# A deeper buffer plan for two interleaved attentions, with the head split of Q moved by small DMAs

## The chip, the cores and the metric

The kernel runs on one core of one Trainium2 chip. Its engines are called PE (matmuls), ACT (exponentials and other functions), DVE (vector work), GpSimd (POOL in profiles) and SyncE (SP in profiles), which here only issues DMA transfers. The metric is the device time of one execution in microseconds (us), the median of several runs. All runs quoted here were in the same, undisturbed state; the granted TensorE clock of each is given where it matters.

## The reference

Two attentions on a sequence of 2048, width 512, 32 heads of 16; the outputs stand side by side. A works on four segments of 512 with a causal mask and a linear memory carried between segments; B is plain attention.

```python
# A, for each segment s of 4 (L = 512)
logits = einsum('bhqd,bhkd->bhqk', qs, ks) * scale + mask
a_dot  = einsum('bhqk,bhkd->bhqd', softmax(logits), vs)
a_mem  = (phi(qs) @ M) / (phi(qs) @ z + 1e-6)       # phi(t) = t+1 if t>0 else exp(t)
o      = g * a_mem + (1 - g) * a_dot                # g = sigmoid(beta), per head
M, z   = M + phi(ks).T @ vs, z + phi(ks).sum()
# B
p = softmax(einsum('bhqd,bhkd->bhqk', q, k) * Dh**-0.5)
o = einsum('bhqk,bhkd->bhqd', p, v)
# both: heads joined, times wo, concatenated on the last axis
```

B has 4 x 4 x 2 x 16 = 512 blocks of exponentials (chunks of queries, rows of heads, halves of a row, blocks of keys), each of four banks of 512 columns in PSUM, the memory that PE writes. B is the greater part of the work.

## The kernel before

The program schedules itself while it is built. It keeps a clock for each engine (`T["pe"]`, `T["dve"]`, `T["sp"]` and so on), prices every operation, and emits instructions in the order that this model gives. Projections, loads and memory updates are "chores" with a due place, an earliest time (`after`) and a condition (`ok`). So a changed rule or price reorders instructions everywhere.

ACT does most exponentials, two or three banks at a time, into "P buffers" (tile pT), from which PE multiplies them with V. Some blocks of B, the "V blocks", are done on DVE instead: four conversions out of PSUM (L938) and three additions (L954) per block, into a ring of buffers (tile vx).

```python
VBUFS = 9        # ring "vx" of the V blocks
VBACK = 1.5      # us of work that may wait for DVE before V scores are refused
PBUFS = 6        # buffers of exponentials
WARMTH = 0.52    # below this activity, PE gets multiplications with zeros

def load_xT(pool, name, ch, tag, bufs):              # x of a segment: four transposing DMAs, SyncE
    t = pool.tile([P, 4, W], BF16, name=f"xT_{name}", tag=tag, bufs=bufs)
    for cc in range(4):
        nc.sync.dma_start_transpose(t[:, cc, :], xs[name][ch * W:(ch + 1) * W, cc * P:(cc + 1) * P])
    return t

# in do_q: Q of two heads comes out of PSUM, then two GpSimd passes by a mask `par`
        def evac():
            qc = wk.tile([P, W], BF16, name="qc", tag="qc", bufs=2)
            pin(nc.vector.tensor_copy(qc[:], ps[:]))
            for e in range(2):
                pin(nc.gpsimd.tensor_scalar(dst[:, e, :], qc[:], par[:, e:e + 1], 0.0, ALU.mult, ALU.add))
                on_pool(0.8, T["dve"])
            mark(key, T["pool"])
# ...
        def seg_chores(s, rt):                        # projections of segment s of A, row of heads rt
            # ...
            def project():
                rel = T["sp"] + 3.5                   # when x is taken to be there
                if (s, rt) != (0, 0):
                    chore(d - LEAD, part(k()), 4, after=rel if s else ARRIVE[...],
                          key=("k", "a", s, rt), ok=lambda: s == 0 or ("phk", s - 1, rt) in seen)
                    chore(d - LEAD, part(q()), 4, after=rel if s else ARRIVE[...],
                          key=("q", "a", s, rt))
                # ... rt == 0: four chores for v
            def load():
                if s > 0:
                    xTA[s] = load_xT(wk, "a", s, "xTA", 1)
                    on_sp(4 * 1.3, T["pe"])
                # ...
                project()
            if rt == 0:
                chore(d - 18, load(), 1, slot=False, ok=...)
            else:
                project()                             # rows 1 to 3: at once, without load()

        def v_pick():                                 # may a block of B go to DVE?
            if vlive[0] > VBUFS - 2:
                return False
            # ...
        def v_scores(taken, lim=2, force=False):
            n = 0
            while n < lim and (force or backlog() < VBACK) and free_slots(...) and v_pick():
                # one score matmul into PSUM; later() queues L938, 0.685 us, on DVE,
                # and three additions L954, 0.70 us each

        def held_back(t):                             # a score step waits for its P buffer
            return pend.get(t - PBUFS, 0) > 0
```

All matmuls go through one helper (`mm`, line 117 of before), so in the profile they carry one line and are told apart by their tiles. PE, DVE, ACT and GpSimd run in program order; SyncE's DMAs are not pinned.

## Time and profile before

| before | value | from |
|---|---|---|
| time | 898.31 us, median of 3 (898.14 to 898.75) | runs |
| granted clock, profiled run | 0.997 | cores |
| ACT busy; exponentials from three or two banks | 868.2 of 896.6 us; 749 | busy times, groups |
| V blocks (512 blocks of B in all) | 124 | groups |
| splits of Q on GpSimd in the run | 28 | groups |

ACT's waits for scores, as the profile gives them (us in total, times, longest):

```profile
ACT pT L865 <- PE s_ps L117: 7.5, 12, 2.0
```

The busy time of one ACT instruction overlaps the next, though (in the changed kernel one starts at 180.60 us and runs 1.58 us, and the next starts at 181.93), so that "97% busy" does not say how near to its own fastest pace ACT runs.

### The profile page before, as it was taken

How to read it: one execution, taken by the hardware profiler on the slowest of the kernel's cores; microseconds unless marked ns; L12 is line 12 of the kernel's file. 1: busy time of each engine (PE TensorE's matmuls, PEld its weight loads, DVE VectorE, ACT ScalarE, POOL GpSimd, SP SyncE). 2: the span in 40 equal slices, each digit the busy share in tenths (PEclk: the TensorE clock that was granted, in tenths of full speed). 3: DMA queues.
4: the chain of work that ended last, by engine and by line, in shares of the span. 5: the costliest groups of instructions: out<-in, count | busy, mean ns of one | idle time of the engine just before them, and what ended most of it. 6: DMA issues, size and time to landing. Idle time of an engine off the chain costs nothing. (4 is left out here: it accounts for less than half of the span.)

```text
span 896.6 us, 18791 instructions
## 1 busy us (share of the span) xinstructions
PE 838.0 (93%) x7541; PEld 259.5 (29%) x7664; DVE 793.5 (88%) x1355; ACT 868.2 (97%) x779; POOL 156.8 (17%) x333
## 2 busy tenths in 40 slices
PE   8899999999999999999999999999999999999995
PEld 3222233322322222223332222223222222223221
DVE  4678799989798998999989998998999899999994
ACT  5999999999999999999999999999999999999995
POOL 5720300421403022031210404012040300000000
PEclk9999999999999999999999999999999999999998
DMA  9600000010000101000000010000000000000000
GB/s 205 129 9 13 18 2 7 7 30 2 7 1 19 37 7 26 1 1 7 2 7 1 20 36 1 1 1 1 2 2 1 14 30 7 1 2 1 1 2 29
DMA packets 36273, 15.48 MB, mean 17 GB/s; under 512 B 27984, under 2 KB 36176, under 8 KB 36176
## 3 DMA queue, kind: packets, MB, share of 16 engines
q1 hardware_dynamic: 34976, 13.78, 6.6%
q8 instruction: 62, 1.02, 0.5%
q10 hardware_dynamic: 1200, 0.39, 0.2%
q14 instruction: 35, 0.29, 0.1%
HBM read 4.20 MB, written 4.19 MB: 9 GB/s over the span
## 5 line engine op out<-in xcount | busy, mean ns | idle before, releaser
L865 ACT ACTIVATE pT<-s_ps 128x1536 bf16<-128x1536 f32 x749 | 856.2, 1292 | 9.9 <-PE s_ps L117 7.5
L938 DVE TENSOR_SCALAR vx<-v_ps 128x512 uint16<-128x512 f32 x496 | 323.3, 684 | 28.8 <-PE v_ps L117 23.8
L117 PE MATMUL s_ps<-qB,KB 32*128 32x512 bf16 x1552 | 251.7, 382 | 19.4 <-ACT pT L865 13.6
L954 DVE TENSOR_SCALAR vx<-vx 128x2048 uint16<-128x2048 uint16 x372 | 244.7, 693 | 2.1 <-PE acc L117 0.5
L117 PE MATMUL acc<-vx,VB 128*32 128x512 f16 x1984 | 178.0, 385 | 3.7 <-issue 2.3
L117 PE MATMUL v_ps<-qB,KB 32*128 32x512 bf16 x496 | 173.2, 382 | 3.5 <-DVE vx L938 1.1
L875 POOL TENSOR_SCALAR_AFFINE_SELECT pT<-pT 128x256 bf16<-128x256 bf16 (+2 forms) x241 | 105.5, 467 | 385.4 <-ACT pT L865 384.8
L117 PE MATMUL acc<-pT,VB 128*32 128x512 bf16 x1552 | 153.1, 387 | 0.7 <-DVE tT L374 0.5
L117 PEld LDWEIGHTS <-KB 32*128 32x128 bf16 x2048 | 84.6, 91 | 236.2 <-issue 229.3
L117 PEld LDWEIGHTS <-VB 128*32 128x32 bf16 x3536 | 73.1, 94 | 157.0 <-issue 146.1
L117 PE MATMUL acc<-zeros 128*128 128x512 bf16 x324 | 108.0, 385 | 3.5 <-issue 3.3
L374 DVE STREAM_TRANSPOSE tT<-acc 128x512 f32<-128x512 f32 x64 | 44.7, 703 | 17.0 <-PE acc L117 16.7
L117 PE MATMUL s_ps<-qA,kA 32*128 32x384 bf16 (+3 forms) x512 | 52.1, 299 | 8.0 <-ACT pT L865 6.2
L117 PEld LDWEIGHTS <-zeros 128*128 128x128 bf16 x420 | 34.0, 98 | 83.9 <-issue 76.2
L274 POOL TENSOR_SCALAR qA<-qc,par 128x512 bf16<-128x512 bf16 x24 | 18.9, 800 | 150.0 <-DVE qc L272 150.0
L117 PE MATMUL acc<-pT,vA 128*32 128x256 bf16 (+3 forms) x512 | 33.1, 305 | 2.9 <-POOL pT L875 1.2
L117 PEld LDWEIGHTS <-kA 32*128 32x128 bf16 x512 | 17.3, 91 | 47.5 <-issue 44.5
L274 POOL TENSOR_SCALAR qB<-qc,par 128x512 bf16<-128x512 bf16 x32 | 22.6, 716 | 14.8 <-DVE qc L272 14.8
L452 DVE CAST osb<-o_ps 128x512 bf16<-128x512 f32 x28 | 19.2, 686 | 5.9 <-PE o_ps L117 5.9
L408 POOL TENSOR_TENSOR tN<-tT,rsum 128x512 bf16<-128x512 f32 x1 | 1.4, 1367 | 130.5 <-DVE rsum L397 130.5
L272 DVE CAST qc<-q_ps 128x512 bf16<-128x512 f32 x28 | 19.1, 682 | 3.3 <-PE q_ps L117 2.6
L117 PE MATMUL k_ps<-xT_a,w_a 128*128 128x512 bf16 x59 | 18.5, 383 | 0.6 <-issue 0.6
(93 smaller groups left out, 425.4 us busy)
## 6 DMA issues: line engine op xcount, KB each, us to landing
out_dram<-osb SPq DMA_DIRECT2D x31, 128.0 KB, 1.7
w_b<-in_B_wqkv_dram SPq DMA_DIRECT2D x3, 512.0 KB, 5.0
phk<-phkT SPq DMA_TRANSPOSE x48, 2.4
w_a<-in_A_wv_dram SPq DMA_DIRECT2D x1, 512.0 KB, 4.5
wo_a<-in_A_wo_dram SPq DMA_DIRECT2D x1, 512.0 KB, 4.6
wo_b<-in_B_wo_dram SPq DMA_DIRECT2D x1, 512.0 KB, 5.3
xT_a<-in_A_x_dram SPq DMA_TRANSPOSE x16, 2.8
w_a<-in_A_wk_dram SPq DMA_DIRECT2D x1, 256.0 KB, 4.7
```

The source lines that it names most:

```text
L117: return pin(nc.tensor.matmul(out, lhsT, rhs, **k))
L272: pin(nc.vector.tensor_copy(qc[:], ps[:]))
L274: pin(nc.gpsimd.tensor_scalar(dst[:, e, :], qc[:], par[:, e:e + 1], 0.0, ALU.mult, ALU.add))
L374: pin(nc.vector.transpose(st["tT"][:, e].rearrange("p c d -> p (c d)"), acc[:]))
L408: pin(eng.tensor_tensor(o, tT[:, :, :, 0:DH], rr.to_broadcast(bc), op=ALU.mult))
L452: pin(nc.vector.tensor_copy(osb[:], ps[:]))
L865: pin(nc.scalar.activation(pT[:, 0:n, :], pt[:, 0:n, :], ACT.Exp, scale=SCALE))
L875: pin(nc.gpsimd.affine_select(out=blk, in_=blk, compare_op=ALU.is_ge, fill=0.0, base=0, pattern=[[0, len(sls)], [1, P]], channel_multiplie ...
L938: pin(nc.vector.tensor_scalar(x[:, j, :], vt[:], XSCALE, float(LADDER[0]), ALU.mult, ALU.add))
L954: pin(nc.vector.tensor_scalar(p[:], x[:], float(off - LADDER[0]), 32767.0, ALU.add, ALU.min))
```

## The change

Its intent: keep more V blocks going and keep GpSimd out of DVE's way. The V rule is relaxed (VBACK), the ring gets a tenth buffer and P buffers rise to eight; to pay for the memory, three of the four x chunks of B live in the ring only while keys and values are projected, and are loaded again for later Q. Q is split by eight small DMAs into tiles that were zeroed once, unless SyncE's queue is late.

```diff
-VBUFS = 9        +VBUFS = 10
-VBACK = 1.5      +VBACK = 1.8
-PBUFS = 6        +PBUFS = 8
-    bd = const.tile([P, 2, P], F32, name="bd")
+    bd = const.tile([P, 2, P], BF16, name="bd")
@@ do_q
-            for e in range(2):
-                pin(nc.gpsimd.tensor_scalar(dst[:, e, :], qc[:], par[:, e:e + 1], 0.0, ALU.mult, ALU.add))
-                on_pool(0.8, T["dve"])
-            mark(key, T["pool"])
+            if live[0] and T["sp"] < T["dve"] + 1.0:
+                for e in range(2):
+                    for j in range(4):
+                        r = slice(32 * j + DH * e, 32 * j + DH * e + DH)
+                        nc.sync.dma_start(out=dst[r, e, :], in_=qc[r, :])
+                        on_sp(0.5, T["dve"] + 0.1)
+                mark(key, T["sp"] + 2.2)
+            else:
+                ... as before
@@ x of B
-        xTB += [load_xT(wk, "b", ch, f"xTB{ch}", 1) for ch in range(1, 4)]
+        xTB += [load_xT(wk, "b", ch, "vx", VBUFS) for ch in range(1, 4)]
+            def again():
+                xTB[ch + 1] = load_xT(wk, "b", ch + 1, "xTB0", 1)
+                on_sp(4 * 1.3, T["pe"])
+                xat[ch + 1] = T["sp"] + 3.5
+            chore(..., q(), ..., ok=lambda: xat.get(ch, 1e9) < T["pe"])
... zeros 128 columns wide and broadcast; Q tiles zeroed once; vlive starts at 5; last store on ACT's queue
```

More of the change, by code (lines that the diff above doesn't have):

```diff
@@ L39 @@
 PREWARM = 16
-VBUFS = 9
+VBUFS = 10
 VMIN = 3
 VLATE = 0.5
-VBACK = 1.5
+VBACK = 1.8
 BANKS = (3, 2)
-PBUFS = 6
+PBUFS = 8
 SWITCH = 0.095
@@ L272, in evac @@
             pin(nc.vector.tensor_copy(qc[:], ps[:]))
-            for e in range(2):
-                pin(nc.gpsimd.tensor_scalar(dst[:, e, :], qc[:], par[:, e:e + 1], 0.0, ALU.mult, ALU.add))
-                on_pool(0.8, T["dve"])
-            mark(key, T["pool"])
+            if live[0] and T["sp"] < T["dve"] + 1.0:
[6 more added lines that the diff above has]
+            else:
+                for e in range(2):
+                    pin(nc.gpsimd.tensor_scalar(dst[:, e, :], qc[:], par[:, e:e + 1], 0.0, ALU.mult, ALU.add))
+                    on_pool(0.8, T["dve"])
+                mark(key, T["pool"])
             if phi is not None:
@@ L487 @@
         ld(nc.sync, 2)
-        xTB += [load_xT(wk, "b", ch, f"xTB{ch}", 1) for ch in range(1, 4)]
+        xTB += [load_xT(wk, "b", ch, "vx", VBUFS) for ch in range(1, 4)]
         woA = load_wo(big, "a", nc.sync)
         woB = load_wo(big, "b", nc.sync)
-        zeros = wk.tile([P, W], BF16, name="zeros")
+        zeros = wk.tile([P, 1, P], BF16, name="zeros")
         nc.gpsimd.memset(zeros[:], 0.0)
+        zcols = zeros[:].to_broadcast([P, 4, P])
         pre = mp.tile([P, W], F32, name="pre", tag="misc")
         for i in range(PREWARM):
-            mm(pre[:], zeros[:, 0:P], zeros[:], start=(i == 0), stop=(i == PREWARM - 1))
+            mm(pre[:], zeros[:, 0, :], zcols, start=(i == 0), stop=(i == PREWARM - 1))
         KB = big.tile([P, NRT, S], BF16, name="KB")
@@ L503 @@
         head_masks()
+        qz = {n: [wk.tile([P, 2, W], BF16, name=f"q{n}{rt}") for rt in range(NRT)] for n in "ab"}
+        for rt in range(NRT):
+            nc.gpsimd.memset(qz["b"][rt][:], 0.0)
         kA, qA, vA, phq, mbds, qB = {}, {}, {}, {}, {}, {}
@@ L537 @@
         okm = wk.tile([P, 2], BF16, name="okm")
-        chores, nchore, seen = [], [0], set()
+        chores, nchore, seen, xat, left_b = [], [0], set(), {0: 0.0}, [0]
         def place():
@@ L560, in q @@
             def q():
-                qA[s, rt] = wk.tile([P, 2, W], BF16, name="qA", tag=f"qA{rt}")
+                qA[s, rt] = qz["a"][rt]
                 if s > 0:
@@ L632, in bq_chores, with q, counted @@
         def bq_chores(ch, rt):
-            qB[ch, rt] = wk.tile([P, 2, W], BF16, name="qB", tag=f"qB{rt}")
-            chore(pos0["b", ch, rt] - LEAD - 1.5, do_q(mp, wk, wB, xTB[ch], rt, qB[ch, rt], None, ("q", "b", ch, rt)),
-                  after=ARRIVE["wvb"], key=("q", "b", ch, rt))
+            qB[ch, rt] = qz["b"][rt]
+            def q():
+                yield from do_q(mp, wk, wB, xTB[ch], rt, qB[ch, rt], None, ("q", "b", ch, rt))
+                if rt == NRT - 1 and ch < NSEG - 1:
+                    chore(pos0["b", ch, rt] - LEAD - 1.0, again(), 1, slot=False, ok=lambda: left_b[0] == 0)
+            def again():
+                xTB[ch + 1] = load_xT(wk, "b", ch + 1, "xTB0", 1)
+                on_sp(4 * 1.3, T["pe"])
+                xat[ch + 1] = T["sp"] + 3.5
+                return
+                yield
+            chore(pos0["b", ch, rt] - LEAD - 1.5, q(), after=ARRIVE["wvb"], key=("q", "b", ch, rt),
+                  ok=lambda: xat.get(ch, 1e9) < T["pe"])
         def b_kv_chores():
-            left = {"k": S // P, "v": S // P}
-            def counted(which, g):
+            left = {"k": S // P, "v": S // P, 1: 8, 2: 8, 3: 8}
+            left_b[0] = 2 * S // P
+            def counted(*keys, g):
                 yield from g
-                left[which] -= 1
-                vlive[0] -= left[which] == 0
+                left_b[0] -= 1
+                for k in keys:
+                    if k:
+                        left[k] -= 1
+                        vlive[0] -= left[k] == 0
             def ones():
@@ L652, in b_kv_chores @@
                     chore(pos0["b", 0, rt] - LEAD - (KLEAD if rt else 0) + 3 * ch,
-                          counted("k", do_k(mp, wB, xTB[ch], rt, KB[:, rt, ch * W:(ch + 1) * W], ("k", "b", ch, rt))),
+                          counted("k", ch, g=do_k(mp, wB, xTB[ch], rt, KB[:, rt, ch * W:(ch + 1) * W], ("k", "b", ch, rt))),
                           after=ARRIVE["xb"][ch], key=("k", "b", ch, rt))
             for sb in range(S // P):
-                chore(pos0["b", 0, 0] - 0.5 + 0.9 * sb, counted("v", do_v(
+                chore(pos0["b", 0, 0] - 0.5 + 0.9 * sb, counted("v", sb // 4, g=do_v(
                     mp, wB, xTB[sb // 4], sb % 4, v_heads(VB, sb)[:, :, 0:DH], ("v", "b", sb))),
@@ L660 @@
         held.update(pk=0, ph=0)
-        vlive, npool = [2], [0]
+        vlive, npool = [5], [0]
         def begin(t):
@@ L1091, in zero @@
                 spare = palloc(mp, [P, W], "spare")
-                mm(spare[:], zeros[:, 0:P], zeros[:], start=True, stop=True)
+                mm(spare[:], zeros[:, 0, :], zcols, start=True, stop=True)
                 slots[slot_of.pop(id(spare))[0]] = T["pe"]
@@ L1095, in zero @@
             for _ in range(n):
-                mm(acc[:], zeros[:, 0:P], zeros[:], start=False, stop=False, skip_group_check=True)
+                mm(acc[:], zeros[:, 0, :], zcols, start=False, stop=False, skip_group_check=True)
             return True
@@ L1107 @@
         kA[0, 0] = wk.tile([P, W], BF16, name="kA", tag="kA0")
-        qA[0, 0] = wk.tile([P, 2, W], BF16, name="qA", tag="qA0")
+        qA[0, 0] = qz["a"][0]
         for cc in range(4):
@@ L1239 @@
             r0 = (NSEG - 1) * W + sb * P
-            (nc.scalar if sb == 2 else nc.sync).dma_start(out=out2[r0:r0 + P, D:2 * D], in_=osb[:])
+            (nc.scalar if sb > 1 else nc.sync).dma_start(out=out2[r0:r0 + P, D:2 * D], in_=osb[:])
     def exact_problem(name):
```

## The prediction

> **What bounds the kernel now.** I read the page in this order: busy times and slices (which engine is full, and when), the costliest groups (what fills it), the waits (whether it ever starves), then stretches of the span engine by engine.
>
> ```profile
> PE 838.0 (93%) x7541; PEld 259.5 (29%) x7664; DVE 793.5 (88%) x1355; ACT 868.2 (97%) x779; POOL 156.8 (17%) x333
> ...
> L865 ACT ACTIVATE pT<-s_ps 128x1536 bf16<-128x1536 f32 x749 | 856.2, 1292 | 9.9 <-PE s_ps L117 7.5
> L938 DVE TENSOR_SCALAR vx<-v_ps 128x512 uint16<-128x512 f32 x496 | 323.3, 684 | 28.8 <-PE v_ps L117 23.8
> ...
> L954 DVE TENSOR_SCALAR vx<-vx 128x2048 uint16<-128x2048 uint16 x372 | 244.7, 693 | 2.1 <-PE acc L117 0.5
> ...
> L117 PE MATMUL acc<-zeros 128*128 128x512 bf16 x324 | 108.0, 385 | 3.5 <-issue 3.3
> ...
> L274 POOL TENSOR_SCALAR qA<-qc,par 128x512 bf16<-128x512 bf16 x24 | 18.9, 800 | 150.0 <-DVE qc L272 150.0
> ...
> L274 POOL TENSOR_SCALAR qB<-qc,par 128x512 bf16<-128x512 bf16 x32 | 22.6, 716 | 14.8 <-DVE qc L272 14.8
> ```
>
> ACT is the bound: 868.2 of 896.6 us, 856.2 of it exponentials, idle only 9.9 us before them, 7.5 of that for scores. PE's 93% is no second bound: 108.0 us of it are multiplications with zeros that the program puts in to keep PE occupied. Nothing can shorten the run much except fewer exponentials on ACT. The program has an outlet for that: some key blocks of B ("V blocks") are exponentiated on DVE instead, by four conversions out of PSUM (L938) and three 16-bit additions (L954), each block then taking four rounds of matmuls with V instead of one. 496/4 = 124 blocks go that way; 372/3 = 124 agrees. So the number of V blocks sets the time, and DVE's free time and the scheduler's rules set that number. All instructions are placed when the program is built, by a model of the engines inside it; so a change of a rule or of a modelled time changes what is scheduled everywhere.
>
> The exchange rate. 124 of B's 4 x 4 x 2 x 16 = 512 blocks are on DVE, 388 on ACT, i.e. 1552 banks of 512 columns (the count of B's score matmuls in the profile); A adds 16 x 20 = 320. 856.2 us / 1872 banks = 0.457 us a bank, so a block moved takes 4 x 0.457 = **1.83 us off ACT**. On DVE it costs (323.3 + 244.7 - overlap) / 124; the windows for the tile vx give 547.1 us of DVE for both groups together, so **4.41 us**. On PE it costs about 4 x 0.35 + 16 x 178.0/1984 = 2.8 us against 4 x 0.16 + 153.1/388 = 1.0 us: 1.8 us more, which the 108 us of zeros can give up.
>
> Where DVE has room. The same row of engines in five stretches:
>
> ```profile
> 750.00:850.00 100.00, 94.70 (x902) 29.24 (x915) 97.00 (x158) 99.45 (x88) 1.37 (x1) 1.00 0.01 1
> ...
> 50.00:175.00 125.00, 119.53 (x992) 37.16 (x1007) 107.35 (x186) 121.30 (x110) 21.83 (x43) 1.00 0.04 10
> 175.00:250.00 75.00, 71.19 (x631) 22.69 (x639) 66.28 (x125) 75.00 (x70) 17.02 (x31) 1.00 0.06 12
> 250.00:750.00 500.00, 472.15 (x4365) 144.84 (x4433) 461.48 (x783) 497.70 (x445) 82.97 (x166) 1.00 0.04 10
> ```
>
> The third figure with a count is DVE. At the end, where only B is left, it reaches 97.0%; before, it idles 17.7 + 8.7 + 38.5 us. Those, with 3.0 at the end, are the 67.9 us that could hold V blocks: 15 at the very most, of which the last 3% cannot be had. DVE's own waits say that it starves for PE's output, not for buffers:
>
> ```profile
> DVE vx L938 <- PE v_ps L117: 23.8, 57, 1.3
> DVE tT L374 <- PE acc L117: 16.7, 9, 4.4
> ```
>
> The 28 two-pass splits of Q on GpSimd matter through this. In the timeline of DVE and GpSimd:
>
> ```profile
> 191.57 1.36 POOL L274 TENSOR_SCALAR qB<-qc,par 128x512 bf16<-128x512 bf16 x2 [2.23 <-DVE qc L272]
> ...
> 190.79 0.68 DVE L272 CAST qc<-q_ps 128x512 bf16<-128x512 f32 x1
> 192.80 0.69 DVE L253 CAST kA<-k_ps 128x512 bf16<-128x512 f32 x1 [1.32 <-PE k_ps L117]
> 193.40 0.68 DVE L954 TENSOR_SCALAR vx<-vx 128x2048 uint16<-128x2048 uint16 x1
> ```
>
> An addition L954 is held until GpSimd is through, DVE standing empty for 1.32 us. It is the program's model that does this (it keeps such additions out of GpSimd's slots, 0.8 us a pass). Windows laid over all 28 splits hold 44.3 us, DVE busy for 34.7: 22% idle against 8.5% in general.
>
> **What the Trainium skill says.** (1) "Perfetto Trace Analysis", Identifying the Most-Contended Engine: occupancy is a fair measure for Vector and Scalar, not for the matmul row. The trace agrees: ACT at 97%, PE's 93% partly zeros. (2) "SBUF - State Buffer", Who interferes with whom: a VectorE operation in a two-port mode and a GpSimd operation exclude each other for a whole instruction, and DMA meets neither. The trace agrees in the tail: L954 has a median of 686 ns and a maximum of 1542. But 372 x (693 - 686 ns) is only 2.6 us, so the real collisions are dear singly and few; the avoidance in the model costs more. (3) "DMA: Bandwidth & Descriptors", Latency and other measured facts: a transfer has some 2 us of fixed cost. The trace agrees: 128 KB stores land in a median of 1.7 us, transposes in 2.4; and each plain issue takes SyncE about 0.5 us in the timeline. (4) Same page, Rules for kernel authors: small transfers pay mostly overhead and are better joined. The change does the opposite, 8 transfers of 16 KB a split; it can afford to only if nobody waits.
>
> **The change part by part.**
> - *Q by DMA.* Some 24 of 28 splits (the early ones find SyncE's queue full and keep GpSimd): 48 passes gone, about 35 us of GpSimd. On DVE nothing is removed, the conversion to qc stays. What is gained is the idle excess, (22% - 8.5%) x 44.3 = 6.0 us, and some 3 us of collisions (2.6 from L954 and a little on two-input operations): **9 us of DVE, about 2 blocks.** It adds 24 x 8 = 192 issues x 0.5 us = 96 us of SyncE, which has hundreds of idle us. Q is ready 8 x 0.5 + 2.2 = 6.2 us after qc instead of 1.4. Its projection is due 4 score steps before use (four banks each, 4 x 1.83 = 7.3 us) and mostly runs earlier as filler, so ACT should not see it; I allow 1 us.
> - *VBACK 1.5 to 1.8.* PE may queue another half L938 ahead for DVE, which goes at the 23.8 us and at the 12.3 us of tT waits that are not the tail. I choose a third to a half of the remaining 67.9 - 9 - 3 = 56 us: **20 us of DVE, 4.5 blocks.**
> - *Buffers.* x of B moves into the ring of vx (9 to 10). While B's keys are projected (the last KB conversion starts at 174.6 us), the ring now also holds three x chunks and one or two weights: 5 or 6 places free, before 7 or 8. In 62 to 175 us the trace has 87/7 = 12.4 V blocks; I take off **1.5**. Afterwards one place more, and 8 P buffers instead of 6 let PE put off matmuls with P: **plus 1**.
> - *x reloaded.* 12 more transposes of some 1.3 us issue on SyncE, asked for a whole row of heads before use (some 50 us): nothing.
> - *Narrow zeros, bd in bf16, the last store on ACT's queue.* Parts of a microsecond; the tail after the last exponential (12 us) stays.
>
> Sum: 2 + 4.5 - 1.5 + 1 = 6 blocks, x 1.83 = 11.0 us off ACT, 1 us given back for Q's lateness: 898.3 - 10 = **888**.
>
> **The rivals.**
> 1. *DVE fills to its ceiling.* If 50 to 750 us also reached 97%, 64.9 - 21 = 44 us would be won, 10 blocks, 18 us: 880, just 2%. For it: 97.0% is reached at the end, and 48.24 of 50 us in the stretch 650 to 700, with units of A among it. Against: 250 to 750 carries masks, transposes and memory updates that come in clumps, and the early ring is tighter.
> 2. *Nothing moves,* since ring and PSUM slots, not the backlog rule, hold V blocks back: 3 PSUM buffers serve projections, V scores and sums alike. DVE's wait for L938 would stay near 24 us and the time at 895 to 898. For it: the ring is worse off early. Against: DVE waits for PE at 57 places, and additions almost never wait.
> 3. *Q comes late.* Eight transfers, behind transposes and stores on one in-order queue, land later than the assumed 2.2 us; PE executes in order, so score steps stop and ACT with them. 28 x 1 us would eat the gain: 898, at 2 us each over 910. For it: the model does not know what the queue really does. Against: 7 us of lead and mostly idle queues (DMA share 0.04).
>
> **Range and chances.** Blocks gained between 2 and 10 cover most outcomes, with 0 to 4 us lost on Q: 881 to 896. Faster by over 2% means under 880.3, which needs rival 1 in full: 0.13. Slower by over 2% needs rival 3 with 40 misplaced microseconds: 0.03. The rest is within 2%.
>
> **What would show it.** L938 count near 520 (130 blocks), L954 near 390, exponentials near 739; DVE about 91%, ACT still 97%; its wait for PE on L938 below 20 us; GpSimd near 120 us with some 8 passes at L274; early blocks (62 to 175 us) fewer than 12.4. It is wrong if the block count stays (rival 2), if ACT's wait for scores grows beyond 12 us (rival 3), or if blocks rise by 10 and more (rival 1).

## The result, and the profile after

The changed kernel took 897.91 us (median; 896.83 to 899.51) beside 898.44 for the kernel before in the same rounds: ratio 0.9995, interval 0.9982 to 1.0008, the same. The prediction, 888 in a range of 881 to 896, was wrong. Ratios are the mean time of one kernel's fast runs over the mean of the other's of the same rounds, so they are not quite the ratio of the medians quoted. Where I turn a ratio into microseconds, it is multiplied by 898.

The page of the changed kernel, its busy times, groups and DMA issues (engine, operation, tiles, count; then busy us and mean ns; then idle time before them):

```profile
PE 863.9 (96%) x7673; PEld 258.9 (29%) x7673; DVE 796.1 (89%) x1362; ACT 866.6 (97%) x777; POOL 130.8 (15%) x295
...
L893 ACT ACTIVATE pT<-s_ps 128x1536 bf16<-128x1536 f32 x747 | 854.9, 1289 | 13.0 <-PE s_ps L117 8.8
L966 DVE TENSOR_SCALAR vx<-v_ps 128x512 uint16<-128x512 f32 x500 | 328.4, 685 | 26.8 <-PE v_ps L117 21.6
...
L982 DVE TENSOR_SCALAR vx<-vx 128x2048 uint16<-128x2048 uint16 x375 | 248.9, 693 | 5.0 <-PE v_ps L117 3.2
L117 PE MATMUL acc<-zeros 128*128 128x512 bf16 x395 | 135.4, 389 | 0.0
...
qb<-qc SPq DMA_DIRECT2D x96, 16.0 KB, 1.8
qa<-qc SPq DMA_DIRECT2D x72, 16.0 KB, 1.8
```

125 V blocks where 124 were: one more, not six. 96 + 72 = 168 small transfers are 21 of the 28 splits. PE's count rises from 7541 to 7673 mostly because the trace of before lacks some matmul records (its weight loads count 7664); the zeros tell the same story, 324 recorded of 403 that the program before emits, so the two PE shares must not be compared. The additions take 693 ns as before, with a quarter of the GpSimd passes: so the 3 us of collisions that the prediction booked did not show as a gain.

The same stretches engine by engine as in the prediction (the third figure with a count is DVE, the fourth ACT; then the clock):

```profile
50.00:175.00 125.00, 122.50 (x1016) 37.36 (x1013) 102.91 (x184) 124.13 (x114) 16.57 (x36) 1.00 0.08 18
175.00:250.00 75.00, 68.12 (x569) 20.07 (x565) 62.61 (x114) 67.00 (x63) 11.68 (x21) 0.93 0.08 18
250.00:750.00 500.00, 488.68 (x4473) 145.94 (x4471) 468.60 (x797) 498.16 (x445) 64.11 (x140) 1.00 0.07 16
```

Early, DVE does less (102.91 against 107.35 us), later more (468.60 against 461.48). The V instructions on DVE alone go from 87 to 79 in 50 to 175 us, from 17 to 8 in 175 to 200, and from 577 to 600 in 200 to 750. The odd row is the second: ACT loses 8.0 us of 75 (75.00 to 67.00), the clock falls to 0.93.

What the engines wait for (engine, tile and line, releaser; us in total, times, longest) says where:

```profile
DVE vx L966 <- PE v_ps L117: 21.6, 54, 3.8
DVE tT L382 <- PE acc L117: 12.4, 8, 5.4
...
ACT pT L893 <- PE s_ps L117: 8.8, 12, 5.0
```

ACT's waits for scores have the sum and the count of before, yet one of the twelve is 5.0 us long, where the longest was 2.0. In PE's order of time around it (start, duration, tiles, count, idle before and its releaser), then ACT's next exponential:

```profile
180.30 0.82 PE L117 MATMUL q_ps<-xT_a,w_a 128*128 128x512 bf16 x3
181.06 0.39 PE L117 MATMUL s_ps<-qb,KB 32*128 32x512 bf16 x2
186.48 0.59 PE L117 MATMUL q_ps<-xT_a,w_a 128*128 128x512 bf16 x1 [5.04 <-DMA xT_a<-in_A_x_dram]
...
187.97 0.61 PE L117 MATMUL s_ps<-qb,KB 32*128 32x512 bf16 x3
```

```profile
188.63 1.45 ACT L893 ACTIVATE pT<-s_ps 128x1536 bf16<-128x1536 f32 x1 [5.02 <-PE s_ps L117]
```

PE stands at the fourth matmul of a Q projection of A's third segment, because the last quarter of that x has not arrived; everything behind it in PE's order stands too. SyncE's DMAs in the same time:

```profile
174.84 3.74 SPq L234 DMA_TRANSPOSE xT_a<-in_A_x_dram  x3
178.68 4.96 SPq L277 DMA_DIRECT2D qa<-qc  x8
183.68 1.26 SPq L234 DMA_TRANSPOSE xT_a<-in_A_x_dram  x1
```

Eight of the new transfers, 0.62 us of issue each, stand between the third transpose and the fourth. After the wait PE's groups take 0.61 us instead of 0.39 until about 195 us. The Trainium skill ("TensorE: Matmul & The Clock Gate", Why this matters for your kernels) warns of PE idling over about 3 us between bursts, because it falls back to the slower clock; the 5.04 us gap and the 0.61 us groups agree, and the clock over 150 to 200 us is 0.90.

What this one stall costs: the program's own model of ACT follows the trace of the changed kernel within 1 us up to exponential 145, at 184 us; five exponentials later, beyond the stall, the trace is 6.9 us late, a jump of 7.8. (From there the gap shrinks to 4.2 us at the last exponential; in the kernel before, the trace gains 4.8 us on the model.) That model ends ACT's work at 889.3 us for the kernel before and at 881.9 us after, 7.4 us earlier. So the change did win some seven microseconds on paper, and one stall of about the same size took them.

In the kernel before, the same x was asked for later and used later, and no one waited: SyncE issues four transposes in a row, and PE's first matmul with them comes 9.0 us later (191.72):

```profile
182.74 5.04 SPq L234 DMA_TRANSPOSE xT_a<-in_A_x_dram  x4
```

Two theories. *Order on SyncE*: the new transfers delay the transposes. *Used too soon*: the program lets rows 1 to 3 of a segment project at `T["sp"] + 3.5` as read when the row's chores are registered, which can be before x of that segment was even asked for; only row 0 hangs on `load()`. In the changed kernel the model asked for x at 178.2 and counted it there at 189.1, yet placed the first Q with it at 181.0 (`after` was 176.5). In the kernel before, x was counted there at 193.5 and first used at 191.8: wrong too, and just near enough.

### The profile page after: what moved, and what is told of

The parts are those of the page before. It is cut to its first block, busy times and chain, and to the rows that moved or that the text cites. A ratio compares the mean times of both kernels' runs of the same rounds, so it can differ in the third digit from the quotient of the medians.

```text
span 897.7 us, 19235 instructions
## 1 busy us (share of the span) xinstructions
PE 863.9 (96%) x7673; PEld 258.9 (29%) x7673; DVE 796.1 (89%) x1362; ACT 866.6 (97%) x777; POOL 130.8 (15%) x295
## 4 chain that ended last, share of the span: by engine, by line
ACT 25%; PE 21%; issue 9%; DVE 5%; POOL 0%; DVEq 0%; ACTq 0%
ACT pT L893 24%; PE acc L117 11%; PE s_ps L117 6%; PE v_ps L117 2%; DVE vx L966 2%; DVE vx L982 2%; PE o_ps L117 1%; DVE tT L382 1%; ACT ex L307 0%; POOL pT L903 0%; PE l_ps L117 0%; PE q_ps L117 0%; DVE OT_b L430 0%; DVE rsum L405 0%; DVE osb L1264 0%
## 5 line engine op out<-in xcount | busy, mean ns | idle before, releaser
L966 DVE TENSOR_SCALAR vx<-v_ps 128x512 uint16<-128x512 f32 x500 | 328.4, 685 | 26.8 <-PE v_ps L117 21.6
L117 PE MATMUL s_ps<-qb,KB 32*128 32x512 bf16 x1548 | 249.4, 384 | 8.2 <-ACT pT L893 4.0
L982 DVE TENSOR_SCALAR vx<-vx 128x2048 uint16<-128x2048 uint16 x375 | 248.9, 693 | 5.0 <-PE v_ps L117 3.2
L117 PE MATMUL v_ps<-qb,KB 32*128 32x512 bf16 x500 | 181.8, 382 | 2.0 <-DVE vx L966 0.9
L117 PE MATMUL acc<-vx,VB 128*32 128x512 f16 x2000 | 180.8, 384 | 2.0 <-DVE vx L982 0.7
L117 PEld LDWEIGHTS <-KB 32*128 32x128 bf16 x2048 | 82.8, 91 | 237.1 <-issue 230.2
L117 PE MATMUL acc<-zeros 128*128 128x512 bf16 x395 | 135.4, 389 | 0.0
L117 PE MATMUL s_ps<-qa,kA 32*128 32x384 bf16 (+3 forms) x512 | 53.3, 299 | 5.3 <-ACT pT L893 3.0
L382 DVE STREAM_TRANSPOSE tT<-acc 128x512 f32<-128x512 f32 x64 | 44.9, 704 | 12.8 <-PE acc L117 12.4
L117 PE MATMUL q_ps<-xT_a,w_a 128*128 128x512 bf16 x64 | 19.8, 386 | 5.0 <-DMA xT_a<-in_A_x_dram 5.0
L117 PE MATMUL o_ps<-wo_a,OT_a 128*128 128x512 bf16 x64 | 18.8, 383 | 0.3 <-DVE vx L966 0.2
```

The lines of the kernel that those rows point to most:

```text
L117: return pin(nc.tensor.matmul(out, lhsT, rhs, **k))
L382: pin(nc.vector.transpose(st["tT"][:, e].rearrange("p c d -> p (c d)"), acc[:]))
L966: pin(nc.vector.tensor_scalar(x[:, j, :], vt[:], XSCALE, float(LADDER[0]), ALU.mult, ALU.add))
L982: pin(nc.vector.tensor_scalar(p[:], x[:], float(off - LADDER[0]), 32767.0, ALU.add, ALU.min))
```

## The experiments

Edits are against the kernel after, unless the text says "on before". "Arrival" is the edit of e1. Block counts are those of the built program.

### Which of the two made the stall

**e1_x_arrival**: after, with an arrival condition for A's x.

```diff
+        xla = {}
 ... k:   ok=lambda: s == 0 or ("phk", s - 1, rt) in seen
 ... k: + and xla.get(s, 1e9) <= T["pe"]
 ... q: + ok=lambda: s == 0 or xla.get(s, 1e9) <= T["pe"]
 ... load():
+                    xla[s] = T["sp"] + 3.5
```

> The changed kernel with one more condition in the scheduler: projections of segment s of A wait, in the scheduler's own clock, until the load of that segment's x, as it books it, has landed (before, only row 0 of the segment did; rows 1 to 3 took the state of the SyncE queue at an earlier moment). Theory 'used too soon': the 5.0 us wait of q_ps for xT_a, and the slow clock after it, vanish although the order on SyncE stays (the fourth transpose still behind eight transfers of Q). 124 V blocks, 749 exponentials, and 5 to 6 us less than the changed kernel: 892.5 us. Rival 'no headroom': the stall is made up elsewhere, since DVE limits the run, and the time stays at 897 to 898.

Measured: 895.36 us, ratio 0.9965 (0.9951 to 0.9979), 124 blocks. PE no longer waits for x of A, although SyncE's order there is the same, transfers between the third and the fourth transpose. But less was won than expected. The profiled run, with 899.28 us at a clock of 0.988 the slowest of six (the rest 894.3 to 895.9), shows a second jam on SyncE. First SyncE, then DVE:

```profile
492.59 2.44 SPq L234 DMA_TRANSPOSE xT_b<-in_B_x_dram  x2
495.14 5.96 SPq L277 DMA_DIRECT2D qb<-qc  x8
501.14 2.56 SPq L234 DMA_TRANSPOSE xT_b<-in_B_x_dram  x2
503.80 3.09 SPq L462 DMA_DIRECT2D out_dram<-osb  x4
```

```profile
505.84 0.69 DVE L460 CAST osb<-o_ps 128x512 bf16<-128x512 f32 x1 [3.99 <-DMA out_dram<-osb]
```

Here stores of results stand behind the reload of B's x and behind eight transfers of Q. DVE waits 3.99 us for a store buffer, PE 4.1 us for DVE, ACT 4.0 us for PE. It is the same queue with another victim. This run also has a stretch of slow clock (0.74 in 700 to 720 us; 0.50 from 706 to 716) for which I have no cause: in the ten microseconds before it, PE's longest gap is 0.35 us.

**e2_x_in_order**: after, with the transposes pinned in program order, so that they are not shuffled among the transfers. The programs of PE, DVE, ACT and GpSimd stay identical.

```diff
-            nc.sync.dma_start_transpose(t[:, cc, :], ...)
+            pin(nc.sync.dma_start_transpose(t[:, cc, :], ...))
```

> The changed kernel with the transposes of x kept in program order on SyncE; all other engines' programs are identical. The four transposes of x of A now stand together, behind the eight transfers of Q instead of around them. Theory 'used too soon': the wait is not cured but grows by some 2 us, since the first three transposes too now start 5 us later; 899 to 900 us. Rival 'the order on SyncE is at fault, the queue was split in the middle of a load': the wait disappears and the time falls to 890 to 891.

Measured: 898.88 us, ratio 1.0011 (0.9998 to 1.0025): nothing won. SyncE, and PE's waits for x:

```profile
175.33 4.94 SPq L277 DMA_DIRECT2D qa<-qc  x8
180.37 5.11 SPq L234 DMA_TRANSPOSE xT_a<-in_A_x_dram  x4
```

```profile
PE q_ps L117 <- DMA xT_a<-in_A_x_dram: 5.1, 3, 3.1
```

In its own order, x comes after the transfers altogether, and PE waits 5.1 us in three pieces instead of 5.0 in one. Program order does not put x first, so this order is no cure. An order with x first was not run. An estimate from the trace of the changed kernel: its fourth transpose started at 183.68 and PE went on 2.8 us later; started right behind the third, at 178.6, it would have landed near 181.4, about when PE came to need it. By this estimate the 5 us there took both, the early use and the transfers in between.

**e11_before_vback18** (on before: `VBACK = 1.8`, nothing else) and **e12_before_vback18_arrival** (the same with the arrival edit). Neither has a single small transfer.

> The kernel before the change with VBACK 1.8 and nothing else. As built: 124 V blocks as before; x of segment 2 of A is asked for at 181.0 us of the scheduler's clock, lands at 193.2 and is used at 183.8. Theory 'used too soon' holds without any Q by DMA: a wait of q_ps or k_ps for xT_a of 5 to 9 us and a slow clock behind it, 904 to 908 us. Rival 'only the transfers of Q make x late': 898 to 899 us.

> The run before it with the arrival condition on x of A. As built: 124 V blocks, 749 exponentials. Theory: no wait for xT_a, and 898 to 900 us, so VBACK 1.8 alone gains nothing; the difference to the run before it is the price of the early use, 6 to 9 us. If VBACK did what the prediction says it would be 890.

Measured: 907.00 us, ratio 1.0122 (1.0094 to 1.015), and 898.14, ratio 1.0009 (0.9993 to 1.0026); 124 blocks each, as in before. The wait that separates them, in e11:

```profile
PE k_ps L117 <- DMA xT_a<-in_A_x_dram: 4.8, 4, 3.1
```

e12 has no such line. So the flaw is the use before arrival; it was in the kernel before, hidden by timing, and VBACK alone brings it out, at a price of 9 to 10 us (8.9 by medians, 10.1 by ratios; one run of e11 took 911.56). The transfers of Q make x later in the kernel after but aren't needed for the flaw. And the expected 4.5 blocks of VBACK are none: same count, same time. (Before with the arrival edit alone was not run.)

### What each part gave

**e3_vback15**: `VBACK` back to 1.5. **e4_q_on_gpsimd**: the branch with small DMAs off (`if False:`), so Q is split on GpSimd as before.

> The changed kernel with VBACK back at 1.5. As built: 123 V blocks (one fewer than before the change, two fewer than after), 751 exponentials, and by chance of the order no early use of xT_a. Theory 'stall and ACT gaps, not blocks, made the time': the time falls though blocks are lost: 894 to 895 us, ACT idle before exponentials 5 us or less, no wait for xT_a. Rival 'the number of V blocks sets the time': two blocks fewer cost 3.7 us, 901 us.

> The changed kernel with all splits of Q on GpSimd as before the change; the rest of the change stays. As built: 123 V blocks, 751 exponentials, x of A asked for 9 us earlier and used after landing. Theory: no wait for xT_a, so about 896 us in spite of two blocks fewer than the changed kernel; that makes Q by DMA worth two blocks (the 3.7 us I predicted for it) and the cause of the stall. Rival 'Q by DMA costs nothing, the reload of x of B stalls': the wait for xT_a stays, 901 us.

Measured: 892.84 us, ratio 0.9941 (0.9928 to 0.9955), and 892.11, ratio 0.9940 (0.9927 to 0.9954). Both have 123 blocks, *two fewer* than the kernel after and one fewer than before, and both beat both. Neither has a wait of PE's matmuls for A's x. Undone together (built, not run) the two edits also give 123: two blocks come only from VBACK and small DMAs jointly.

**e5_pbufs6**: e4 with `PBUFS = 6`. It holds all of the change but the small DMAs and the P buffers.

> The changed kernel with Q on GpSimd (as in the fourth run) and with 6 P buffers again. As built: 123 V blocks and 751 exponentials, exactly as in the fourth run; only the order on PE differs. Theory 'the eight P buffers are what closed ACT's gaps': the gaps near 19 and 111 us come back, ACT idles 8 to 9 us inside the run instead of 3, and the time rises by 4 to 5 us over the fourth run, to 896 to 897 us. Rival 'the ring or VBACK closed them': 892 us.

Measured: 901.16 us, ratio 1.0043 (1.0031 to 1.0055), 123 blocks. ACT's waits for scores, first in e5 with six buffers, then in e4 with eight:

```profile
ACT pT L893 <- PE s_ps L117: 5.8, 14, 1.4
```

```profile
ACT pT L893 <- PE s_ps L117: 1.7, 4, 0.9
```

With the same 751 exponentials, two P buffers are worth (1.0043 - 0.9940) x 898 = 9.2 us in this pair of programs. They do not bring blocks; by the program's rule (`held_back`) they let PE run score steps on without first finishing the matmuls that empty a P buffer. The listed waits fall by 4.1 us only; the excess over ACT's own pace, explained below, falls by 8.1 (29.7 to 21.6).

This gives the ledger of the change by ratios, in this order of steps: everything but small DMAs and P buffers +3.9 us; P buffers -9.2; small DMAs (e4 to after, 0.9940 to 0.9995) +4.9; together -0.4. In the first term, one block fewer accounts for 1.8 us by the exchange rate; the rest of it I did not separate.

The last term is not a price of the small DMAs as such. e3 keeps 152 of them (88 + 64) and is as fast as e4, so with VBACK as the last step the same 4.8 us would stand against VBACK. The cost shows where the two stand together; with both undone the kernel was not run. Of the 4.9 us, 2.7 go when A's x is waited for (e1 against after); 2.2 remain (e1 against e4, whose schedule the arrival edit does not change when it is built with it), though e1 has a block more.

**e10_pbufs10**: e4 with arrival, `PBUFS = 10` and `VBUFS = 9`.

> The fourth run's kernel (Q on GpSimd) with 10 P buffers and 9 places in the ring, and the arrival condition. As built: 124 V blocks, 749 exponentials. Theory 'P buffers are what pays in this change': two buffers more and one block more give 2 to 4 us below the fourth run's 892, 888 to 890 us. Rival 'eight are enough': 891 to 892 us.

Measured: 891.18 us, ratio 0.9927 (0.9910 to 0.9943), 124 blocks. It is the fastest correct kernel here, but its interval overlaps that of e4; two further P buffers at the price of one ring buffer are not shown to help.

### Would more V blocks have paid

The prediction took every block for 1.83 us. To buy blocks, the price of DVE work in the program's model is lowered:

```diff
+DSCALE = 0.95
 ... later():
-        tasks.append(dict(..., us=us, ...))
+        tasks.append(dict(..., us=us * DSCALE, ...))
```

**e6_dve_price95** is e4 with arrival and 0.95, **e7_dve_price92** the same with 0.92, **e8_before_price95** is on before, with arrival and 0.95.

> The fourth run's kernel with the scheduler's price of every DVE task times 0.95 (L938's step from 0.630 to 0.596 us; in the trace the start-to-start step of such instructions is 0.60), and the arrival condition on x of A. As built: 130 V blocks, 739 exponentials. Theory 'the number of V blocks is set by the price that the scheduler books for DVE, which is too high, not by DVE, by VBACK or by the ring': seven blocks more, 7 x 1.83 = 12.8 us less than the fourth run's 892: 879 to 880 us, DVE at 92%. Rival 'PE or DVE cannot take more': exponentials wait for scores, time 888 or more.

> As the run before it with the price times 0.92, below what the trace shows (0.575 us against 0.60). As built: 133 V blocks, 735 exponentials. Theory: a price that is too low makes PE wait for DVE in places; 3 more blocks are worth 5.5 us at most, so 874 if DVE still has room, and above 880 if the limit has been reached. I expect 876.

> The kernel before the change, with the price of DVE tasks times 0.95 and the arrival condition on x of A, nothing else. As built: 129 V blocks, 741 exponentials. Theory: five blocks more than before, 9.2 us less, and ACT's gaps near 6 us as before: 888 to 889 us, without anything of the change. Rival 'blocks need the larger ring and more P buffers': 895 us or more.

Measured: 897.22 us with 130 blocks, ratio 0.9992 (0.9979 to 1.0005); 914.07 with 133, ratio 1.0176 (1.0162 to 1.0190); 901.18 with 129, ratio 1.0031 (1.0018 to 1.0044). My theory at this point, that blocks are the currency and the program's rules hold them back, fell: seven blocks more than e4 cost (0.9992 - 0.9940) x 898 = 4.7 us instead of bringing 12.8. The busy times of e4 and e6:

```profile
PE 848.7 (95%) x7595; PEld 259.4 (29%) x7649; DVE 787.5 (88%) x1348; ACT 869.1 (98%) x781; POOL 160.7 (18%) x338
```

```profile
PE 862.2 (96%) x7692; PEld 255.9 (29%) x7692; DVE 812.4 (91%) x1397; ACT 863.7 (96%) x769; POOL 158.3 (18%) x337
```

ACT has twelve exponentials fewer to do and is done later. From the start of an exponential to the start of ACT's next instruction, the least time is 1.330 us for three banks and 0.904 for two within 3 ns in every trace here, 0.447 a bank. What all exponentials together take above these minima, called the excess here, is 27.8 us in before, 29.9 in after, 21.6 in e4, 29.7 in e5, 40.3 in e6 and 63.4 in e7. So the blocks are paid for in ACT's pace. Two of PE's waits grow, first in e6, then in e4:

```profile
PE acc L118 <- DVE vx L985: 2.7, 9, 0.6
PE v_ps L118 <- DVE vx L969: 2.3, 12, 0.3
```

```profile
PE acc L117 <- DVE vx L982: 0.5, 2, 0.2
PE v_ps L117 <- DVE vx L966: 0.4, 2, 0.2
```

All of PE's waits for DVE, its weight loads included, rise from 13.0 us to 22.1. One reading is that PE meets a matmul that needs DVE's result, stands, and the scores behind it come late. e8 speaks against this as the whole story: there the same waits are 18.9 us, beside 18.5 in before, and five blocks more still cost time.

A rival stays untested. Every run with more blocks got them by a lower price, so more blocks and a model that is too hopeful came together. Built again with its clock written out, the model ends the exponentials of e4 at 887.2 us and the trace at 879.1, 8.1 earlier; in e6 it says 873.8, and the trace ends 11.0 later, at 884.8. No run raised the count at the old price.

**e9_price95_few_zeros** asks whether the zeros on PE are in the way: e6 with `WARMTH` 0.52 to 0.40, so that 122 multiplications with zeros are left of 360.

> The sixth run's kernel (DVE price times 0.95, 130 V blocks, which came out at 897 and not at 880) with the threshold for multiplications by zeros at 0.40 instead of 0.52. As built: 131 V blocks, 738 exponentials, 122 multiplications by zeros instead of 360. Theory 'PE took the place of DVE as the limit: the seven extra blocks' matmuls stand in one in-order queue with the zeros and delay the scores': 238 zeros fewer x about 0.3 us leave PE some 70 us of slack, the waits of exponentials shrink, 882 to 886 us, if the granted clock stays at 0.99 or above. Rival 'it is DVE's lateness, which PE waits for': 895 us or more at full clock. If the clock falls below 0.97 the run decides nothing.

Measured: 894.03 us, ratio 0.9949 (0.9917 to 0.9982), 131 blocks. Inconclusive: one run took 889.38 at a clock of 0.998, three took 893.6 to 895.2 at 0.987. Fewer zeros came with a lower clock in three runs of four; the one at full clock, 7.8 us below e6, fits a gain from time on PE.

**e13_price95_half_pv** and **e14_half_pv** take work from PE without touching the schedule: the matmuls of V blocks with V run on half their columns, in e6 and in e4 with arrival. The results are wrong (relative errors 0.31 and 0.30).

```diff
 def mm(..., half=False):
+        if half:
+            n = out.free_size() // 2
+            out, rhs = out[:, 0:n], rhs[:, 0:n]
```

> The sixth run's kernel (130 V blocks, 897 us) with the matmuls of V blocks with V done on half their columns, except the first and last of a sum; wrong results on purpose, the order of all instructions and all of DVE's and ACT's work unchanged. It takes about a tenth of a microsecond off some 490 rounds on PE, up to 50 us. If PE is what the seven extra blocks ran into: 884 to 887 us, the excess of ACT's start-to-start steps (41 us there, 21 us in the fourth run) falls to 25 us or less. If it is DVE's lateness, which PE waits for in order: 893 us or more, with PE's waits for DVE grown.

> The control: the same halving on the fourth run's program (123 V blocks, 892 us); wrong results on purpose. If PE has slack there, nothing changes: 890 to 892 us. If PE holds ACT up there too, it falls as much as the run before it.

Measured: 889.23 us, ratio 0.9903 (0.9885 to 0.9921), and 885.50, ratio 0.9872 (0.9856 to 0.9889). By ratios, relief on PE is worth 8.0 us with 130 blocks (against e6) and 6.1 with 123 (against e4, whose schedule the arrival edit does not change). So PE holds ACT back in both, in spite of its zeros; but of the 17.5 us by which e6 misses its exchange rate (12.8 + 4.7), that explains only 8.0 - 6.1 = 1.9. By an estimate it may be near 4: three of e13's runs had a clock of 0.993 to 0.994, and its one run at 0.997 took 887.35. The rest remains where PE is relieved: e13 is still 2.8 us slower than e14 with 12 exponentials fewer, and its excess is 30.8 us, not the 25 expected, beside 15.2 in e14. The remainder goes with PE's waits for DVE, 26.2 us in e13 and 12.4 in e14; that DVE causes it is not shown, for no run made DVE faster, and the price too low is the rival said above.

**e15_pbufs10_price97**: e10 with a price of 0.97.

> The best version so far (10 P buffers, ring of 9, Q on GpSimd, 891 us) with the price of DVE tasks times 0.97. As built: 128 V blocks, 743 exponentials. If a moved block pays in full as long as few are added: 4 x 1.8 = 7 us less, 884 us. If blocks beyond about 124 are lost again, as the sixth run says: 889 to 893 us.

Measured: 898.83 us, ratio 1.0003 (0.9977 to 1.0029), with 128 blocks. Ten P buffers don't rescue the extra blocks either: four more than e10, and 6.8 us slower. Two of its runs had a clock of 0.992; the two at 0.996 and 0.997 (897.29 and 895.87) are still 5 to 6 us slower than e10.

## Why the prediction was wrong

The step that failed is the one from the relaxed rules to six more V blocks and from blocks to time. One block came, not six; and where the count moved, the time did not follow it: e4 with two blocks fewer than after is 4.9 us faster, e6 with seven more than e4 is 4.7 us slower. Term by term:

- *ACT is the bound; a block moved takes 1.83 us off it.* The bound is right. The rate is right as an amount of work: the least pace of 0.447 us a bank makes it 1.79. As an exchange rate for time it failed beyond some 124 blocks (e6, e7, e8, e15). The step from "DVE idles 68 us" to "some of it can be had" is the one that broke: the blocks could be had at a lower price (130 in e6, DVE at 91%), but ACT's excess grew by 18.7 us. Whether that is because DVE's idle time between jobs lets PE find its results ready, or because the lowered price misleads the scheduler, is open.
- *Q by DMA: about 2 blocks, and 1 us allowed for lateness.* The step that failed was "SyncE, which has hundreds of idle us". 21 splits went to DMA, near the 24 said, and the two blocks came, though only jointly with VBACK. But what counts is who stands in the queue at one moment: in a stall of 5.0 us x waited, in e1 stores. Against e4 the DMAs cost 4.9 us with VBACK at 1.8 in place of a gain of 2.7 (2 x 1.83 - 1), and 2.2 where A's x is waited for. Three sizes were off besides: an issue took 0.62 us, not 0.5; the 4 score steps of lead hold for Q of B, while the code gives A's Q 2.5 (4.6 us); and the 1.32 us that the prediction put down to GpSimd are, in the line shown, a wait of DVE for PE's k_ps.
- *VBACK: 4.5 blocks.* Failed. Alone on before it gives none (e11, e12), jointly two. By itself it also brought out the flaw in the arrival of x, for 9 to 10 us.
- *Buffers: minus 1.5 blocks early.* About right: 8 instructions fewer on DVE in 50 to 175 us, 8/7 = 1.1 blocks. Another 9/7 = 1.3 went in the 25 us of the stall.
- *P buffers: plus 1 block with the ring.* The largest mis-sized term: 9.2 us, and not through blocks. The prediction's list of ACT's waits was 9.9 us long, and I took it for too small to matter; the summed excess over ACT's own minimum, 27.8 us in before, is what there was to win, and e4 takes 6.2 of it with a block fewer.
- *x reloaded, "nothing".* True of the wait for x of B: no trace looked at for this shows one. But its transposes helped to fill the queue of e1.
- *Rival 2, nothing moves,* gave the time (895 to 898), and DVE's wait for L938's input stayed near 24 us as it said (21.6). But nothing moving was a sum of -9.2 and two losses, not stillness: that the rival's number came true is luck. *Rival 3* had the right mechanism, PE in order and one queue, with x as the late one instead of Q. The test that I set for it, ACT's wait for scores above 12 us, missed it: that wait is 8.8. The longest single wait showed it, not the total.

## What to carry to other kernels

Before moving work onto a DMA queue, list what else is issued on it at the same moments and who waits for that; a queue idle for hundreds of microseconds can still be five late where it counts. Give every consumer a condition on the actual arrival of its data: a release time guessed from another event works until any unrelated rule shifts the schedule. When a change moves nothing, undo its parts one at a time before believing in a lever: here one part was worth 9 us and the others spent it.

## What the Trainium skill lacked or had wrong

- "DMA: Bandwidth & Descriptors", Issuing engines are not separate DMA queues, says that the sequencer time to initiate a DMA is usually small relative to the DMA itself. For 16 KB transfers it is not: eight took 4.96 us to issue, 0.62 each, beside 1.8 us each from issue to landing, and the transpose behind them started 5.1 us after the three before them ended (178.58 to 183.68; PE then waited 5.04 us). The page does not give the cost of such a queue to the others in it.
- "Perfetto Trace Analysis", Identifying the Most-Contended Engine, calls occupancy a fair measure of the distance to roofline for Vector and Scalar. For ACT it was too kind here: in before, at 97%, its exponentials took 27.8 us above their least start-to-start times (1.330 and 0.904 us), of which only 11.9 show as idle time; the rest lies inside busy time, since an instruction's busy time overlaps the next one's.
- Too few buffers are named in the skill as a possible cause of gaps, but no page says what a deeper set between ACT and PE is worth: 9.2 us from six to eight (e5, e4), nothing shown from eight to ten (e10).
